# A three-stage attention and expert kernel on one core: where its made weights are split, staged and loaded

## The chip, the cores and the metric

The kernel runs on one NeuronCore of one Trainium2 chip. The metric is the time of one execution in device microseconds, as the median of several runs; a profile is one further execution taken by the hardware profiler. TensorE (PE in the profile) multiplies matrices, VectorE (DVE), ScalarE (ACT) and GpSimd (POOL) work elementwise, and SyncE (SP) issues nearly all transfers here, in program order. Each engine runs its own instructions in order and waits on semaphores for the others.

## The reference

Attention over 8 heads and 8 batches between 512 rows x and 32 state rows, both ways, gives 544 rows for each batch. They are laid side by side (4608 tokens, 512 features) and go through two expert layers, all in float32:

```python
def _moe_ref(x, w_gate, w_val, w_out):          # 512 -> 1536 -> 512
    gate = 1.0 / (1.0 + np.exp(-(x @ w_gate)))
    val = x @ w_val
    return (gate * val @ w_out)

def _moe2_ref(x, w_in, w_out):                  # 512 -> 2048 -> 512
    h = x @ w_in
    g = np.where(h >= 1, h, np.where(h <= -1, 0.0, (h + 1) ** 2 / 4))
    return (g @ w_out)
```

## The kernel before, in words

Every float32 product is three products of a high part and a remainder (hi x hi, hi x lo, lo x hi). So each operand is *split*: ScalarE writes the high part (a copy to the type of the product), VectorE subtracts it from the source and leaves the remainder in place. Several of the large products use a scheme of seven products of sums in place of eight (M1 to M7), for which sums of blocks of the weights and of the activations are made first.

The order of the work is written out by hand. The stages that the change touches, in order of time:

**The value stage, `gated(1, None, hooks)`.** Gate and value product for the second four batches, in 24 units i (L609 on TensorE). A unit uses both PSUM buffers of one of two sets, by turns; `evac1` empties unit i during unit i+1: for even i ScalarE's sigmoid (L638), for odd i VectorE's product (L640), after which POOL makes sums (L220) and `put_h` (L620, its transfer is L622) stores the pieces to `h7_dram`, some of them two units later (`late_st`). Pair products for later units (`m_pair`, L576; ScalarE L588, VectorE L594) and a preparation of raw weights (`weights.join`, L166 and L170) run in between. Into this stage `hooks` puts, by unit: `combos_wo` (L879), which loads rows of `w_out`, makes block sums and stores seven pieces to `wc_dram`; `load_wc`, `high_wc`, `low_wc` (L858 to L878), which load a piece's weights in three parts, and split them, for M1 and M5; and the first three chunks of the next stage's activations (`load_h7`, L916).

**The output product, `out7` (L948), 42 steps n.** Step n takes product j = PP[n // 3 % 7] and chunk c = n % 3. Chunk n+5 is loaded, chunk n+2 is split (L927, L220), then come the 12 matmuls. Weights of the later products are loaded and split in between (`todo`). M1, M5, M2 and M4 have weights in the tiles `wo_0` to `wo_11`, three each, in the order of `HR4`; tiles 6 and 7 also serve `evac1` as scratch, tiles 8 to 11 serve `combos_wo`.

**The state units, `gated_s(m)`, m = 0 to 11 (L1010).** The same gate and value product for the 256 state rows: 24 matmuls (L225 to L227) with weights `ws`, then sigmoid (L1019), product (L1020), split, and for odd m a difference with its split. In the loop (L1898 to L1908) each turn loads unit m+3's weights, runs `gated_s(m)`, splits the weights of unit m+1 (L1004 and L220), runs the `todo` of that turn, and from m = 3 on adds 12 matmuls of the output product for the state rows (`out1_s`, L1044). The `todo` prepares the input weights 0 to 3 of the next stage (`load_wi`, `sums_wi`, `high_wi`, `low_wi`, L1064 to L1092: two blocks of `w_in`, four sums, a split; the sums lie in one scratch tile `wst`) and loads and sums the first inputs y.

**The input product, `unit(b, m)` (L1298).** Ten blocks of four units: with weights 0 to 3, and then with 4 to 7, over the batch pairs 0, 1, 2, the state rows ("s") and pair 3. A unit is seven pieces, and after each piece `tick` runs what `plan` put there. Weights 4 to 7 are prepared as above, one after the other, in the fifth and sixth block (L2023 to L2026); y's sums and remainders for the next block are on POOL.

After it, the second output product (L1366 to L1368) takes the rest of the span.

## Time and profile before

| | us |
|---|---|
| median of 3 runs | 1450.81 (1450.1 to 1451.48) |
| the profiled execution | 1451.23 |
| its span, first to last instruction | 1449.4 |
| TensorE's matmuls busy | 1376.6 (95% of the span) |
| VectorE busy | 978.3 (67%) |
| ScalarE busy | 770.6 (53%) |
| GpSimd busy | 332.5 (23%) |

Busy times are unions of an engine's instructions; matmuls are pipelined, so a busy TensorE can still run slower than at its best. "Clock" is the TensorE clock that was granted, as a share of full speed. A row of waits gives for whom, on whom, the total, the number of times and the longest. Idle time counts only where it holds up the engine that sets the end.

### The profile page before, as it was taken

What the parts mean: (1) busy time and instruction counts of PE and PEld (TensorE: products, weight loads), DVE (VectorE), ACT (ScalarE), POOL (GpSimd) and SP (SyncE); (2) the same over time, 40 slices, a digit from 0 to 9 for tenths busy, and PEclk for the clock granted to TensorE, in tenths of its full rate; (3) what the DMA queues carried; (4) which work ended last, traced back from release to release, by engine and by line L of the source; (5) the groups of instructions that cost most, each with busy time, mean ns of one, the idle gap of its engine ahead of it and who ended that gap; (6) DMA issues with size and microseconds to landing.
All of it is one profiled execution on the core that took longest, in us unless ns stands there. A gap on an engine that the chain in (4) does not pass through costs nothing. (4 is left out here: it accounts for less than half of the span.)

```text
span 1449.4 us, 23550 instructions
## 1 busy us (share of the span) xinstructions
PE 1376.6 (95%) x8956; PEld 1168.1 (81%) x8956; DVE 978.3 (67%) x1377; ACT 770.6 (53%) x1138; POOL 332.5 (23%) x207
## 2 busy tenths in 40 slices
PE   8999999999999989996779999889999999999997
PEld 5677787787677768886668887668889999999997
DVE  6666766774476657454566666986668887877775
ACT  7655556654333445432347786768876444444432
POOL 3000000000053350000027777588741000000000
PEclk9999999999999999997889999999999999999999
DMA  7478897787499898765235555546668534433332
GB/s 254 150 257 287 289 338 239 246 283 260 166 335 341 305 310 307 239 213 169 61 109 202 200 230 197 201 161 233 236 230 319 175 123 141 138 124 117 121 127 88
DMA packets 179634, 308.80 MB, mean 213 GB/s; under 512 B 15040, under 2 KB 101824, under 8 KB 179008
## 3 DMA queue, kind: packets, MB, share of 16 engines
q1 hardware_dynamic: 178712, 306.50, 62.0%
q8 instruction: 70, 1.15, 0.3%
q10 hardware_dynamic: 808, 0.79, 0.2%
q14 instruction: 44, 0.36, 0.1%
HBM read 184.29 MB, written 122.95 MB: 212 GB/s over the span
## 5 line engine op out<-in xcount | busy, mean ns | idle before, releaser
L1298 PE MATMUL u<-yc,wt 128*128 128x512 f32 x1344 | 312.1, 393 | 20.9 <-DVE sg L1276 13.7
L1298 PEld LDWEIGHTS u<-yc,wt 128*128 128x128 f32 x1344 | 253.8, 190 | 78.4 <-DVE sg L1276 14.4
L609 PE MATMUL ps<-at_hi,M 128*128 128x512 f32 x768 | 244.6, 394 | 2.5 <-DVE M L594 2.0
L609 PEld LDWEIGHTS ps<-at_hi,M 128*128 128x128 f32 x768 | 144.9, 189 | 52.1 <-issue 18.4
L609 PE MATMUL ps<-at_lo,M 128*128 128x512 f32 x384 | 150.6, 392 | 1.8 <-DVE at_lo L405 1.8
L1368 PE MATMUL o<-wt,hc 128*128 128x256 f32 x476 | 134.8, 283 | 0.7 <-DVE hc L1415 0.7
L1366 PE MATMUL o<-w,hc 128*128 128x256 f32 x476 | 134.7, 283 | 0.0
L1367 PE MATMUL o<-w,hc 128*128 128x256 f32 x476 | 134.7, 283 | 0.0
L1367 PE MATMUL o<-wt,hc 128*128 128x256 f32 x476 | 134.7, 283 | 0.0
L1368 PE MATMUL o<-w,hc 128*128 128x256 f32 x476 | 134.7, 283 | 0.0
L1366 PE MATMUL o<-wt,hc 128*128 128x256 f32 x476 | 134.7, 283 | 0.0
L1411 ACT ACTIVATE hc<-hc 128x512 fp32r<-128x512 f32 (+1 forms) x108 | 64.9, 603 | 129.9 <-DMA hc<-hd_dram 117.3
L1220 POOL TENSOR_TENSOR yc<-yr,yc 128x1024 fp32r<-128x1024 f32 x49 | 119.6, 2475 | 24.5 <-ACT yc L1217 24.5
L594 DVE TENSOR_TENSOR M<-ps,M 128x1024 fp32r<-128x1024 f32 x48 | 56.5, 1219 | 88.1 <-ACT M L588 88.1
L1258 DVE SCALAR_TENSOR_TENSOR sg<-u,sg 128x512 f32<-128x512 f32 x96 | 66.3, 690 | 61.3 <-ACT u L1257 60.2
L1411 ACT ACTIVATE hc<-hs 128x512 fp32r<-128x512 f32 (+1 forms) x144 | 80.0, 598 | 50.5 <-DVE hs L1408 49.9
L1256 ACT ACTIVATE u<-sg,half 128x512 f32<-128x512 f32 x96 | 66.3, 691 | 70.2 <-DVE sg L1276 68.5
L220 POOL TENSOR_TENSOR sa<-sa 128x512 f32<-128x512 f32 x12 | 17.5, 1479 | 361.2 <-DVE sa L640 355.7
L220 POOL TENSOR_TENSOR w2c<-w2c 128x256 f32<-128x256 f32 (+2 forms) x40 | 43.9, 1111 | 227.6 <-ACT yc L1217 218.7
L1415 DVE TENSOR_TENSOR hc<-hs,hc 128x512 fp32r<-128x512 f32 (+1 forms) x144 | 90.3, 660 | 5.3 <-ACT hc L1411 5.2
L1368 PEld LDWEIGHTS o<-wt,hc 128*128 128x128 f32 x476 | 91.4, 192 | 0.9 <-DVE hc L1415 0.9
L1366 PEld LDWEIGHTS o<-wt,hc 128*128 128x128 f32 x476 | 91.4, 192 | 0.0
(195 smaller groups left out, 3042.9 us busy)
## 6 DMA issues: line engine op xcount, KB each, us to landing
hd_dram<-sg SPq DMA_DIRECT2D x64, 512.0 KB, 4.5
hc<-hd_dram SPq DMA_DIRECT2D x96, 256.0 KB, 4.3
hq<-h_dram SPq DMA_DIRECT2D x39, 512.0 KB, 5.3
yr<-y_dram SPq DMA_DIRECT2D x32, 512.0 KB, 6.6
wraw<-in_moe_w_out_dram SPq DMA_DIRECT2D x28, 512.0 KB, 5.2
h_dram<-sg SPq DMA_DIRECT2D x24, 512.0 KB, 4.3
oh_lo<-h_dram SPq DMA_DIRECT2D x24, 512.0 KB, 5.8
w2c_dram<-w2c SPq DMA_DIRECT2D x12, 896.0 KB, 6.0
```

The source lines that it names most:

```text
L220: eng.tensor_tensor(out=o, in0=a, in1=b, op=op)
L594: nc.vector.tensor_tensor(out=M[:, 1], in0=ps, in1=f32(M[:, 0]), op=ALU.subtract)
L609: nc.tensor.matmul(out=ps[bp][:, b2], lhsT=M[:, l, b2, c], rhs=a[:, b2], start=(hq == 0 and j == 0), stop=(hq == 1 and j == 2),)
L1220: low_on.tensor_tensor(out=t[:, 1, :n], in0=src, in1=f32(t[:, 0, :n]), op=SUB)
L1256: nc.scalar.activation(out=s, in_=c, func=AF.Relu, bias=half, scale=0.5)
L1258: return lambda: nc.vector.scalar_tensor_tensor(out=o, in0=s, scalar=1.0, in1=c, op0=ALU.min, op1=ALU.max)
L1298: nc.tensor.matmul(out=pm[j], lhsT=a, rhs=b, start=not more and k == 0 and i == 0, stop=k == 1 and i == 2, skip_group_check=more,)
L1366: nc.tensor.matmul(out=ps, lhsT=wh, rhs=vh, start=start and i == 0, stop=False)
L1367: nc.tensor.matmul(out=ps, lhsT=wh, rhs=vl, start=False, stop=False)
L1368: nc.tensor.matmul(out=ps, lhsT=wl, rhs=vh, start=False, stop=last)
L1411: nc.scalar.activation(out=get(j)[0], in_=raw(j), func=AF.Copy)
L1415: nc.vector.tensor_tensor(out=lo, in0=raw(j), in1=f32(hi), op=SUB)
```

## The change

- **State units:** unit m+2's weights are split in turn m, not unit m+1's. The scratch tile of the input weights gets a second buffer (every other unit's lies in `hsp`), the two state results share one tile `evs`.
- **Input weights 4 to 7** are loaded, summed and split earlier by `finish_wi`: two in the value stage (in the tiles `wo_8` to `wo_11`), two in the output product (in a pool `wg` of their own). Both parts are stored to `wi_dram`, and the input product loads them as they are, with one transfer of 14 KB a partition.
- **Output product:** `HR4` is M1, M5, M4, M2, so that M2 has tiles 9 to 11; its load and split come in units 20 and 23 of the value stage. Chunks 3 to 7 are loaded before the stores that the last unit of the value stage left, chunk 8 after them. The combinations move to earlier units, and only four of their seven pieces are stored; M1, M2 and M4 are read from the raw rows (`wof_dram`, one tensor now), two rows of 1 KB.
- **Layout:** `h7_dram` is piece first, so a chunk's load reads 4 KB in a row for each partition, where it read two rows of 2 KB; M2's and M3's common store becomes two rows of 2 KB.
- The state rows' input (`load_xs`) is loaded and split six steps later; the pools of the state units open at step 28, not 2.

```diff
@@ -107,8 +107,8 @@
     h_dram = tc.dram_tile([128, NM1, 4, S], F32, name="h_dram")
-    h7_dram = [tc.dram_tile([128, NQ, 7, S], F32, name=f"h7_dram_{p}") for p in range(2)]
-    wc_dram = tc.dram_tile([128, 7, NQ, 256], F32, name="wc_dram")
+    h7_dram = [tc.dram_tile([128, 7, NQ, S], F32, name=f"h7_dram_{p}") for p in range(2)]
+    wc_dram = tc.dram_tile([128, 4, NQ, 256], F32, name="wc_dram")
     xs_dram = tc.dram_tile([128, 4, NSB], F32, name="xs_dram")
@@ -119,7 +119,8 @@
     ]
-    wof_dram = {i: tc.dram_tile([128, 512], F32, name=f"wof_dram_{i}") for i in range(NM1)}
+    wof_dram = tc.dram_tile([128, NM1, 512], F32, name="wof_dram")
+    wi_dram = {m: tc.dram_tile([128, 14, 256], F32, name=f"wi_dram_{m}") for m in range(4, 8)}
     w2_dram = [tc.dram_tile([128, 512], F32, name=f"w2_dram_{i}") for i in range(NM2)]
@@ -618,7 +619,7 @@
     def put_h(p, q, j, a, n=1, due=None):
-        o = h7_dram[p][:, q, HS[j]] if n == 1 else h7_dram[p][:, q, HS[j] : HS[j] + n]
+        o = h7_dram[p][:, HS[j], q] if n == 1 else h7_dram[p][:, HS[j] : HS[j] + n, q]
         f = lambda: nc.sync.dma_start(out=o, in_=a)
@@ -628,7 +629,7 @@
             if v == 0 and mm == 0:
-                sa_t[t] = sgp.tile([128, 3, 512], F32, tag="sa", name="sa", bufs=4)
+                sa_t[t] = (sgp, sgq)[t].tile([128, 3, 512], F32, tag="sa", name="sa", bufs=2)
             elif v == 0:
@@ -730,7 +731,8 @@
         prev()
-        flush()
+        if not bg:
+            flush()
@@ -743,14 +745,14 @@
         def dst(a=None):
-            return wo_tiles(i) if a is None else wof_dram[i]
+            return wo_tiles(i) if a is None else wof_dram[:, i]
...
     def load_wo(i):
-        nc.sync.dma_start(out=f32(wo_tiles(i)[1]), in_=wof_dram[i])
+        nc.sync.dma_start(out=f32(wo_tiles(i)[1]), in_=wof_dram[:, i])
@@ -852,7 +854,9 @@
-    HR4 = (M1, M5, M2, M4)
+    HR4 = (M1, M5, M4, M2)
+    WR = {M1: (0, 0), M2: (1, 0), M4: (1, 1)}
+    WS = {M5: 0, M7: 1, M6: 2, M3: 3}
     wc_t = {}
@@ -863,9 +867,13 @@
         for p in range(3):
+            if j in WR:
+                k, v = WR[j]
+                o = wof_dram[:, 4 * p + k : 4 * p + k + 3 : 2, 256 * v : 256 * v + 256]
+            else:
+                o = wc_dram[:, WS[j], 2 * p : 2 * p + 2]
             nc.sync.dma_start(
-                out=f32(wc_t[j][1][p]),
-                in_=wc_dram[:, WI[j], 2 * p : 2 * p + 2].rearrange("p q f -> p (q f)"),
+                out=f32(wc_t[j][1][p]).rearrange("p (q f) -> p q f", q=2), in_=o
             )
@@ -883,7 +891,7 @@
             for i in range(2):
-                nc.sync.dma_start(out=box[i], in_=wof_dram[2 * q + i])
+                nc.sync.dma_start(out=box[i], in_=wof_dram[:, 2 * q + i])
@@ -894,15 +902,10 @@
         def store():
-            for t, o in zip(box, (slice(0, 4, 3), slice(1, 3), slice(4, 6))):
+            for o, a in enumerate((box[0][:, 256:], box[2][:, :256], box[2][:, 256:], box[3][:, :256])):
                 stores.append(
-                    lambda t=t, o=o: nc.sync.dma_start(
-                        out=wc_dram[:, o, q], in_=t.rearrange("p (s f) -> p s f", s=2)
-                    )
+                    lambda o=o, a=a: nc.sync.dma_start(out=wc_dram[:, o, q], in_=a)
                 )
-            stores.append(
-                lambda: nc.sync.dma_start(out=wc_dram[:, 6, q], in_=box[3][:, :256])
-            )
@@ -920,7 +923,7 @@
         h7_t[n] = t
-        nc.sync.dma_start(out=f32(t[:, 1]), in_=h7_dram[p][:, 2 * c : 2 * c + 2, HS[j]])
+        nc.sync.dma_start(out=f32(t[:, 1]), in_=h7_dram[p][:, HS[j], 2 * c : 2 * c + 2])
@@ -1047,7 +1050,7 @@
         if q == NQ - 1:
-            t = hsp.tile([128, 2, NSB], F32, tag="evs", name="evs", bufs=2)
+            t = hsp.tile([128, 2, NSB], F32, tag="evs", name="evs", bufs=1)
             if half == 0:
@@ -1061,9 +1064,63 @@
+    def finish_wi(m, tiles):
+        box = []
+
+        def r(i):
+            return box[0][1][:, 256 * i : 256 * i + 256] if len(box[0]) == 2 else pieces(i)
+
+        def parts():
+            if len(box[0]) == 2:
+                return [(box[0][0][:, :1792], box[0][1][:, :1792])]
+            n = (512, 512, 512, 256)
+            return [(box[0][p][:, :k], box[0][4 + p][:, :k]) for p, k in enumerate(n)]
+
+        def pieces(i):
+            return box[0][4 + i // 2][:, 256 * (i % 2) : 256 * (i % 2) + 256]
+
+        def load():
+            box.append(tiles())
+            for n, (i, h) in enumerate(((0, 0), (0, 1), (1, 1), (1, 0))):
+                c = slice(256 * h, 256 * h + 256)
+                nc.sync.dma_start(out=f32(r(n)), in_=wir_dram[2 * m + i][:, c])
+
+        def sums():
+            a = [f32(r(i)) for i in range(7)]
+            tt(nc.vector, a[4], a[0], a[3])
+            tt(nc.vector, a[3], a[3], a[2], ADD)
+            tt(nc.vector, a[5], a[3], a[0])
+            tt(nc.vector, a[6], a[1], a[5])
+
+        def high():
+            for hi, lo in parts():
+                nc.scalar.activation(out=hi, in_=f32(lo), func=AF.Copy)
+
+        def low():
+            for hi, lo in parts():
+                tt(nc.vector, lo, f32(lo), f32(hi))
+
+        def store():
+            o = 0
+            for p, (hi, lo) in enumerate(parts()):
+                n = hi.shape[1] // 256
+                for l, a in enumerate((hi, lo)):
+                    stores.append(
+                        lambda l=l, a=a, o=o, n=n: nc.sync.dma_start(
+                            out=wi_dram[m][:, 7 * l + o : 7 * l + o + n],
+                            in_=f32(a).rearrange("p (s f) -> p s f", s=n),
+                        )
+                    )
+                o += n
+
+        return load, sums, high, low, store
+
     def load_wi(m):
         t = w_t[m] = w_tile()
-        wst_t[m] = wst.tile([128, 4, 256], F32, tag="wst", name="wst")
+        if m >= 4:
+            nc.sync.dma_start(out=f32(t).rearrange("p l s f -> p (l s) f"), in_=wi_dram[m])
+            return
+        wst_t[m] = (hsp if m % 2 else wst).tile([128, 4, 256], F32, tag="wst", name="wst")
         nc.sync.dma_start(
@@ -1786,6 +1843,7 @@
+    sgq = pool("sgq", side="right", stack=st_a)
     mp = pool("mp1", side="right", stack=st_a)
@@ -1796,15 +1854,26 @@
-    for q in range(NQ):
+    for q, i in enumerate((0, 1, 3, 4, 6, 7)):
         load, sums, store = combos_wo(q)
-        hook(2 * q, load)
-        hook(2 * q + 2, sums)
-        hook(2 * q + 3, store)
+        hook(i, load)
+        hook(i + 2, sums)
+        hook(i + 2, store)
+
+    def wi_pieces():
+        t = [wo_tiles(8 + i) for i in range(4)]
+        return [a[0] for a in t] + [a[1] for a in t]
+
+    for m, i in ((4, 10), (5, 15)):
+        for k, f in enumerate(finish_wi(m, wi_pieces)):
+            hook(i + (0, 1, 2, 2, 3)[k], f)
+    for k, j in enumerate((M1, M5, M2)):
+        hook((13, 14, 20)[k], load_wc, j)
     for k, j in enumerate((M1, M5)):
-        hook(15 + k, load_wc, j)
         for p in range(3):
-            hook(17 + 3 * k + p, lambda j=j, p=p: (high_wc(j, p), low_wc(j, p)))
+            hook((18, 19, 20, 21, 21, 22)[3 * k + p], lambda j=j, p=p: (high_wc(j, p), low_wc(j, p)))
+    for p in range(3):
+        hook(23, lambda p=p: (high_wc(M2, p), low_wc(M2, p)))
     hook(20, load_h7, 0)
@@ -1817,18 +1886,26 @@
-    st_l, st_sb, st_w, st_e = (ExitStack() for _ in range(4))
+    st_l, st_sb, st_w, st_e, st_g = (ExitStack() for _ in range(5))
     hq = pool("hq", stack=st_l)
...
-    for k, j in enumerate(PP[2:]):
-        do(3 * k + (k == 0), load_wc, j)
+    for k, j in enumerate(PP[3:], 1):
+        do(3 * k, load_wc, j)
         for p in range(3):
...
             do(3 * k + 4, low_wc, j, p)
+
+    def wi_whole():
+        t = wgp.tile([128, 2, 1792], F32R, tag="wg", name="wg", bufs=2)
+        return [t[:, 0], t[:, 1]]
+
+    for m, n in ((6, 14), (7, 20)):
+        for k, f in enumerate(finish_wi(m, wi_whole)):
+            do(n + (0, 3, 4, 4, 5)[k], f)
@@ -1839,18 +1916,24 @@
     global_xs = []
-    do(20, load_xs)
-    do(23, lambda: nc.scalar.activation(out=global_xs[0], in_=f32(global_xs[1]), func=AF.Copy))
-    do(24, lambda: tt(nc.vector, global_xs[1], f32(global_xs[1]), f32(global_xs[0])))
+    do(26, load_xs)
+    do(28, lambda: nc.scalar.activation(out=global_xs[0], in_=f32(global_xs[1]), func=AF.Copy))
+    do(29, lambda: tt(nc.vector, global_xs[1], f32(global_xs[1]), f32(global_xs[0])))
     for m in range(3):
...
         do(36 + 2 * m, low_ws, m)
-    load_h7(3)
-    load_h7(4)
+    for n in range(3, 8):
+        load_h7(n)
+    flush()
+    load_h7(8)
     for n in range(42):
-        if n + 5 < 42:
+        if n == 28:
+            st_g.close()
+            hsp = pool("hsp", side="right", stack=st_sb)
+            wsps = [pool("wsp", side="right", stack=st_w, bufs=3)]
+        if 8 < n + 5 < 42:
             load_h7(n + 5)
@@ -1858,6 +1941,7 @@
             f()
+        flush()
         if n + 2 < 42:
@@ -1866,8 +1950,7 @@
             wcx = pool("wcx", stack=st_l)
-            hsp = pool("hsp", side="right", stack=st_sb)
-            wsps = [pool("wsp", side="right", stack=st_w, bufs=3)]
+            wgp = pool("wgp", side="right", stack=st_g)
         evac7(n)
@@ -1886,7 +1969,7 @@
-    wi = {m: wi_steps(m) for m in range(8)}
+    wi = {m: wi_steps(m) for m in range(4)}
     todo = {}
@@ -1899,9 +1982,9 @@
         gated_s(m)
-        if 0 < m and m + 1 < NM1:
-            high_ws(m + 1)
-            low_ws(m + 1)
+        if m + 2 < NM1:
+            high_ws(m + 2)
+            low_ws(m + 2)
         for f in todo.pop(m, ()):
@@ -2021,9 +2104,7 @@
     for i in range(4):
-        t = start[4] + 9 + 7 * i + 7 * (i == 3)
-        for k, n in enumerate((0, 5, 6, 7, 8)):
-            plan(t + n, wi[4 + i][k])
+        plan(start[4] + 9 + 7 * i + 7 * (i == 3), lambda i=i: load_wi(4 + i))
     for i in range(3):
...
         plan(t, lambda i=i: load_w2(i))

```

## Rows read from the trace of the kernel before

**Rows 1.** Stage windows: length, busy us by engine (xinstructions), PEclk, DMA share, GB/s

```profile
445.00:523.00 78.00, 78.00 (x461) 58.42 (x441) 51.89 (x49) 33.86 (x42) 35.46 (x25) 1.00 0.91 315
...
522.80:646.60 123.80, 117.84 (x506) 96.35 (x505) 71.93 (x68) 56.38 (x62) 8.00 (x6) 0.97 0.81 268
...
541.70:548.60 6.90, 5.74 (x13) 4.22 (x14) 5.30 (x6) 4.66 (x7) 0.00 (x0) 0.51 1.00 347
...
646.50:735.40 88.90, 64.80 (x391) 60.51 (x390) 42.02 (x66) 26.12 (x44) 0.00 (x0) 0.81 0.36 107
...
734.70:740.40 5.70, 5.70 (x50) 5.70 (x48) 3.22 (x8) 2.67 (x5) 0.00 (x0) 1.00 0.02 3
```

**Rows 2.** Waits of TensorE, whole span: us in total, times, longest

```profile
PE ps L225 <- ACT ws L1004: 13.6, 9, 2.5
...
PE u L1298 <- DVE sg L1276: 13.7, 6, 4.6
...
PE ps L948 <- ACT hq L927: 4.6, 1, 4.6
```

**Rows 3.** Waits of SyncE's queue, 500 to 552, then 646 to 741 us

```profile
SPq L866 <- DMA h_dram<-wo: 4.7, 2, 3.2
...
SPq L1070 <- DVE wt L220: 41.3, 3, 17.8
```

**Rows 4.** Timeline of the output product: start, length, engine, line, what, idle

```profile
539.38 2.01 ACT L873 ACTIVATE wo<-wo 128x512 fp32r<-128x512 f32 x3 [5.66 <-DMA wo<-wc_dram]
...
541.29 1.99 ACT L927 ACTIVATE hq<-hq 128x1024 fp32r<-128x1024 f32 x2
```

**Rows 5.** Timeline of the state units

```profile
650.01 0.42 DVE L1020 TENSOR_TENSOR sgs<-sgs,ps 128x256 f32<-128x256 f32 x1 [2.06 <-ACT sgs L1019]
...
702.49 0.42 DVE L1020 TENSOR_TENSOR sgs<-sgs,ps 128x256 f32<-128x256 f32 x1 [1.74 <-ACT sgs L1019]
...
705.58 1.23 DVE L220 TENSOR_TENSOR ws<-ws 128x1024 fp32r<-128x1024 f32 x1 [0.52 <-ACT ws L1004]
...
712.38 0.42 DVE L1020 TENSOR_TENSOR sgs<-sgs,ps 128x256 f32<-128x256 f32 x1 [4.44 <-ACT sgs L1019]
...
714.23 1.23 DVE L220 TENSOR_TENSOR ws<-ws 128x1024 fp32r<-128x1024 f32 x1 [0.52 <-ACT ws L1004]
...
735.36 0.42 DVE L1020 TENSOR_TENSOR sgs<-sgs,ps 128x256 f32<-128x256 f32 x1 [1.20 <-ACT sgs L1019]
...
742.20 3.12 SPq L1055 DMA_DIRECT2D y_dram<-evs  x2
...
745.12 2.47 PE L1298 MATMUL u<-yc,wt 128*128 128x512 f32 x5 [4.52 <-ACT yc L1217]
```

**Rows 6.** Groups of instructions in the state units: busy us, mean ns, idle

```profile
L220 DVE TENSOR_TENSOR wst<-wst,wt 128x256 f32<-128x256 f32 x8 | 3.4, 425 | 0.3
...
L220 DVE TENSOR_TENSOR wt<-wst,wt 128x1024 fp32r<-128x1024 f32 x3 | 3.7, 1218 | 0.0
...
L220 DVE TENSOR_TENSOR wt<-wt 128x768 fp32r<-128x768 f32 x3 | 2.9, 951 | 0.0
...
L220 DVE TENSOR_TENSOR yr<-yr 128x1024 f32<-128x1024 f32 x4 | 4.8, 1218 | 0.0
...
L1086 ACT ACTIVATE wt<-wst 128x1024 fp32r<-128x1024 f32 x4 | 4.2, 1058 | 8.3 <-DVE wst L220 8.3
```

**Rows 7.** Page, DMA issues: count, KB each, us to landing

```profile
hd_dram<-sg SPq DMA_DIRECT2D x64, 512.0 KB, 4.5
```

**Rows 8.** Input product's matmuls by windows: PE, PEld, PEclk, DMA share, GB/s

```profile
778.52:816.60 38.08, 38.08 (x169) 31.54 (x168) 1.00 0.56 204
...
894.78:969.82 75.04, 60.79 (x253) 47.65 (x252) 0.98 0.49 172
```

**Rows 9.** VectorE's groups, 875 to 956 us

```profile
L220 DVE TENSOR_TENSOR wst<-wt,wst 128x256 f32<-128x256 f32 x8 | 12.7, 1583 | 0.1
```

**Rows 10.** Timeline of VectorE in the value stage

```profile
454.89 1.40 DVE L220 TENSOR_TENSOR wo<-wo 128x256 f32<-128x256 f32 x1
```

## The prediction, made before the change was built

> **What bounds the kernel now.** I read the stages first, then the waits of TensorE, then, in each stage with waits, what the waited-for engine was doing. A stage is bounded by TensorE where the windows show no gap in its busy time, and by something else where they do. The value stage (second half batch, up to 522.8) has none in its last 78.00 us. The output product with chunks (522.8 to 646.6) is busy 117.84 of 123.80 us, and the state units (646.5 to 735.4) only 64.80 of 88.90, at a mean granted clock of 0.81 [rows 1]. The list of waits names the causes: weights of the state units (ACT ws 13.6 us), the chunk of the output product (ACT hq 4.6, once), and VectorE's sums in the input product (DVE sg 13.7, six times) [rows 2]. Those three are what the change goes at; the rest of the span is TensorE's own work, and is worth nothing to it.
>
> **Output product: one chain of waits goes.** The second input M2's weights share tiles 6 and 7 with scratch of the value stage. SyncE held their load until the scratch had been stored (4.7 us [rows 3]). ScalarE, in order, then split M2's weights from 539.38 and only at 541.29 the chunk that TensorE stood for [rows 4]. After that stop the clock was granted at 0.51 for 6.90 us [rows 1], the 1.2 GHz level, which costs half of it, 3.4 us. The change gives M2 the tiles 9 to 11, loads it in unit 20 of the value stage, splits it in unit 23, and issues chunks 3 to 7 before the late stores. I take the whole wait and its half clock: -(4.6 + 3.4) = **-8.0**. What is late next is chunk 8, which now waits on SyncE for M2's own last store; only the six late stores stand behind it, and step 8 comes over 20 us into the stage. VectorE gets three remainders of M2 ahead of chunk 1's; if they run slow beside POOL, up to 5 us come back, so the bounds are -9 and -3.
>
> **State units: the splits leave TensorE's loop.** Now, unit m+1's weights are split after unit m's sigmoid, product and splits, so TensorE waits for that chain and then adds its own unit. From the product's start to the end of the weights' remainder the chain takes 706.81 - 702.49 = 4.3 us in an odd unit (it has the difference too) and 715.46 - 712.38 = 3.1 in an even one [rows 5]. Splitting unit m+2 there lets TensorE run unit m+1 meanwhile. Its floor is then 12 x 24 + 8 x 12 = 384 matmuls up to the last product; 48 take 5.70 us at full clock [rows 1], so 46 us. But the in-order chain on ScalarE and VectorE remains, and I find it longer than that. Between the first product and the last one (units 0 to 10) it needs: five odd units 5 x 4.3 = 21.6; five even ones 5 x 3.1 = 15.4; unit 10, with no weights left to split, about 1.3 (a product, a split and its remainder of 0.4 each); three sets of input-weight sums, 3 x 4 x 0.42 = 5.1, and ScalarE's split of them, 3 x 1.06 = 3.2, which stands before the next sigmoid; three sets of remainders, 3 x (1.22 + 0.95) = 6.5; four sums of y, 4 x 1.22 = 4.9 [rows 6]. That is 58.0 against 735.36 - 650.01 = 85.4 measured [rows 5], -27.4. Loads of units 3 to 5 still queue behind wide y loads at the start, so I take **-26**. The bounds: VectorE's own busy time in the stage is 42.02 us [rows 1], which with no wait at all inside the chain would give -43; and no gain, below. The second change here is small in code and needed: SyncE stood 41.3 us for the one scratch tile of the input weights [rows 3], with state weights queued behind it; a second tile removes that, and without it the loads would come too late for a split two ahead.
>
> The clock speaks against this sum. The stage's mean is 0.81 [rows 1], between the levels of 1.2 and 2.4 GHz, so it spent some 40% at the lower one; my chain leaves TensorE waiting some 1 to 2 us in most units. The Trainium skill (TensorE: Matmul & The Clock Gate, HAM oscillation) says that a loop whose waits return in every tile can start every tile at the half clock. By that rule the stage would be bounded by TensorE and hardly change, a rival below. I stay with the chain, because a TensorE at half clock lets the chain catch up, the next wait goes, and the clock returns.
>
> The tail from the last product to the first input product (735.36 to 745.12) is a chain of its own that the change leaves, but for one thing: the two state outputs now share one tile, so the second copy out of PSUM waits until the first one's store has landed. It is issued at 742.20 [rows 5]. A 512 KB store lands in 4.5 us [rows 7], this one is half that size. Bounds 0 (landed in time) and +2.5; I take **+0.7**, since most of a short landing has passed when the copy comes up.
>
> **Input product: four weights' preparation goes.** Undisturbed, four units take 38.08 us, so six take 57.12; the six from 894.78 took 75.04 [rows 8], 17.9 too long, half clock included. In that stretch VectorE makes the weights of units 4 to 7, with 8 of the sums alone taking 12.7 us at 1583 ns each, beside POOL [rows 9]. Afterwards one load brings them ready made. It is 1.84 MB instead of 0.52, four times, 5.3 MB more over 75 us, on DMA engines that are 0.49 busy there [rows 8]; each is issued 12 to 19 pieces ahead of its unit (a unit has seven). I take **-17**, bounds -18 and -12 (if a late load or slow y sums keep a third).
>
> **Value stage: the work moved in.** Two of the four sets are made here, at units 10 to 14 and 15 to 19; M2's split is added in unit 23, and the combinations of the output weights move forward. A set costs VectorE four sums and four remainders, 1.7 + 2.2 us by the free durations [rows 6], but a 256-wide sum beside POOL takes 1.40 [rows 10]. From 445 to 523 VectorE is 51.89 of 78.00 us busy [rows 1], so the time is there. The order is the problem: VectorE comes to the sums one unit after SyncE was to load their inputs, and SyncE takes those loads behind the stores of that unit. If VectorE stands there for a landing, the remainders of the pair products behind it hold PSUM that TensorE needs for its next unit. Bounds 0 (loads land in time) and +10 (two landings of 4.5, exposed, and a little more); I take **+4**, half of a landing for each set. DMA there is 0.91 busy at 315 GB/s [rows 1], so full load is about 346. The window gets some 4 MB more on 24.6 (two loads of 0.52, two stores of 1.84, M2's 0.79, less 1.5 of combinations): 28.6 MB, or 83 us of DMA in 78. That lateness of 5 us lands on the first chunks, whose loads the change puts ahead of the stores, and five steps of lead take it.
>
> The other two sets are made in the output product, where VectorE is busy 71.93 of 123.80 us [rows 1] and two chunks ahead: nothing. The 4 KB rows, the combined tensors and the later pools: nothing, none stands in a chain above; 1 KB rows of three raw weight loads likewise.
>
> **Sum.** The profiled execution took 1451.23 us, 0.4 above the median of the runs. -8.0 - 26 + 0.7 - 17 + 4 = -46.3: 1404.9, or **1404.5** against the median.
>
> **Rivals.**
> 1. *The half clock keeps the state units* (chance 0.08). 384 matmuls at twice 0.119 are 91 us: no gain there, rather +3. For it: 0.81 now. Against: above. Time 1404.5 + 29 = 1434.
> 2. *VectorE stalls the value stage* (0.12). Two exposed landings, each followed by a spell of half clock, +18 instead of +4: 1418.
> 3. *The input product's waits stay* (0.07): it wouldn't do what it says if POOL's y sums, not the weights, are what VectorE is slow beside. The gain there falls to 6: 1415. Against: other units with the same POOL work run at 38.08 per four [rows 8].
> 4. *VectorE and ScalarE overlap better* than my chain in the state units (0.06): -38 there, 1392.
> 5. *Slower* (0.03): SyncE is in order, and in the value stage each of eight load groups (six combinations, two sets) may stand behind the landing of a store issued just before it, with job and pair weights queued behind. To eat 46 us each must cost TensorE 5.8, more than a landing of 4.5 [rows 7]; it decides from there: some 1455.
>
> **Numbers.** Forecast 0.64. The range 1394 to 1426 takes in the forecast with its bounds, and rivals 2 and 3; left out are rival 1, 4 and 5, 0.17. About 0.2% is what a measurement of this kernel tells from no change. Faster 0.96, same 0.01, slower 0.03.
>
> **What would show it.** Right: in the state units the waits for ws are gone or under half, VectorE's last product comes near 709, and SyncE no longer waits for wt; no wait of TensorE for hq near step 5; six units of 57 to 58 us at what is now 895; a few short waits around units 13 and 18 of the value stage. Wrong: a clock near 0.6 throughout the state units; waits for M or ps of several us in the value stage; a wait on the copy before the first input product of over 2 us more.

## The result, and the profile after

The changed kernel takes 1413.59 us (median of 4 executions, 1407.81 to 1414.27) beside 1451.14 for the kernel before on the same chip: a ratio of 0.9729, 95% interval 0.9699 to 0.9759. That is 37.6 us less. The forecast was 1404.5, range 1394 to 1426. The profiled execution took 1414.27, its span is 1412.5.

I cut both spans at the same places: last matmul of the first batches' output product (its end, 364.4 before, 364.5 after), first matmul of `out7`, its last one, first and last of the input product. The last columns split the output product: TensorE starts a matmul every 0.227 us there (the median), so 504 need 114.4 us, and what each group of steps takes beyond that pace is listed, in us. All kernels of this study stand here, so that each can be read by stage; "time" is the median, and a profile is one execution of it.

| kernel | time | value | output | state + tail | input | steps 0-3 | 4-6 | 7-13 | 21-29 |
|---|---|---|---|---|---|---|---|---|---|
| before | 1451.1 | 158.4 | 123.9 | 98.4 | 351.2 | 1.2 | 8.3 | 0.0 | 0.0 |
| changed | 1413.6 | 165.5 | 124.0 | 71.0 | 334.8 | 0.7 | 0.0 | 5.0 | 3.7 |
| one | 1440.1 | 165.3 | 124.8 | 97.6 | 332.9 | 1.3 | 0.0 | 6.4 | 2.6 |
| wst1 | 1412.5 | 165.6 | 124.7 | 71.7 | 332.4 | 0.5 | 0.0 | 7.2 | 2.6 |
| nowi | 1419.8 | 154.8 | 121.5 | 72.1 | 353.3 | 1.8 | 0.0 | 5.3 | 0.0 |
| w67 | 1412.8 | 154.8 | 124.1 | 70.7 | 342.0 | 2.2 | 0.0 | 5.0 | 2.4 |
| rows2 | 1414.0 | 166.1 | 123.5 | 70.9 | 335.2 | 0.0 | 0.0 | 5.9 | 2.6 |
| set2 | 1409.5 | 157.7 | 128.7 | 71.5 | 332.5 | 5.1 | 0.0 | 6.7 | 2.4 |
| wi7 | 1412.8 | 163.9 | 122.9 | 71.4 | 332.5 | 0.1 | 0.0 | 7.0 | 1.3 |
| m6 | 1410.3 | 164.6 | 121.6 | 72.4 | 334.7 | 0.7 | 0.0 | 4.4 | 2.0 |
| ahead | 1412.0 | 165.1 | 122.3 | 70.7 | 332.3 | 4.6 | 0.0 | 0.0 | 3.2 |
| mix | 1408.6 | 165.5 | 120.0 | 70.7 | 333.3 | 0.8 | 2.8 | 0.0 | 1.9 |
| best | 1404.9 | 157.3 | 125.3 | 70.9 | 332.6 | 9.4 | 0.0 | 0.0 | 1.5 |
| best2 | 1404.4 | 158.4 | 123.0 | 71.4 | 333.4 | 7.6 | 0.2 | 0.0 | 0.7 |

Before to after: value stage +7.1, output product +0.1, state units and tail -27.5, input product -16.5. The windows of the changed kernel, as in [rows 1] and [rows 8] (length, busy us by engine, clock, DMA share, GB/s), first the last 78 us of the value stage, then the output product, the state units and six units of the input product:

```profile
452.00:530.00 78.00, 71.30 (x393) 52.82 (x394) 54.02 (x56) 34.50 (x46) 34.67 (x24) 0.96 0.86 303
530.00:654.00 124.00, 118.67 (x507) 96.61 (x506) 80.89 (x77) 57.22 (x61) 10.41 (x6) 0.97 0.85 301
653.80:709.90 56.10, 46.79 (x364) 44.13 (x362) 36.45 (x60) 24.54 (x42) 0.00 (x0) 0.99 0.55 169
...
869.00:926.10 57.10, 57.10 (x253) 47.30 (x252) 36.36 (x55) 44.37 (x66) 47.79 (x24) 1.00 0.94 331
```

The value stage, which had no gap in its last 78 us before, now has 6.7 us of them. The state units run at a clock of 0.99 in this window; a spell of 3.4 us at the lower level (709.3 to 712.7) falls behind its end, and up to the last product (715.2) the mean is 0.97. The six units have no gap left, where [rows 8] had 14 us of them (the window shown begins 30 matmuls early; counted by matmuls the same six run from 876.02 to 933.14, 57.1 us as well), and VectorE is busy 36.36 of 57.10 us without the weights. The list of TensorE's waits (total, times, longest) names what is new:

```profile
PE ps L610 <- DVE M L595: 5.7, 1, 5.7
PE ps L228 <- DVE ws L221: 5.4, 8, 0.8
PE u L1355 <- ACT yc L1274: 5.2, 1, 5.2
PE ps L226 <- ACT ws L1007: 3.8, 4, 1.6
PE ps L951 <- DVE hq L221: 2.6, 2, 1.8
PE ps L951 <- ACT hq L930: 2.3, 1, 2.3
PE u L1355 <- DVE sg L1333: 2.3, 2, 2.0
...
PE ps L610 <- DVE oh_lo L641: 1.7, 1, 1.7
```

Against [rows 2], ScalarE's `ws` fell from 13.6 us to 3.8 and VectorE's `sg` from 13.7 to 2.3. One wait for `hq` of 4.6, with two short ones for VectorE beside it (1.4 in all), has become three of 2.3, 1.8 and 0.8, and two waits in the value stage, of 5.7 and 1.7, are new. With three of them (the 5.7 from 487.13 on, the 2.3 from 552.63 and the 1.8 from 604.23) the clock went to its lower level, 1.2 GHz; these are the windows of those stretches:

```profile
490.80:497.70 6.90, 4.90 (x12) 3.84 (x13) 6.83 (x11) 3.06 (x6) 0.00 (x0) 0.51 0.47 176
555.70:559.10 3.40, 2.89 (x7) 2.31 (x8) 3.40 (x6) 1.20 (x2) 0.00 (x0) 0.50 1.04 396
606.90:610.30 3.40, 3.40 (x10) 2.62 (x9) 3.40 (x3) 3.40 (x4) 0.00 (x0) 0.50 1.05 431
```

The timeline of the changed kernel (start, length, engine, line, what, idle before it) gives two of the causes. VectorE stood 12.29 us for the loads of weight 5 in the value stage, with the small part of M behind them in its queue, and 5.95 us for those of weight 7 in the output product, with a chunk's low part behind:

```profile
483.43 2.08 SPq L1086 DMA_DIRECT2D wo<-wir_dram  x4
...
489.80 0.42 DVE L221 TENSOR_TENSOR wo<-wo,wo 128x256 f32<-128x256 f32 x1 [12.29 <-DMA wo<-wir_dram]
...
491.53 2.35 DVE L595 TENSOR_TENSOR M<-ps,M 128x1024 fp32r<-128x1024 f32 x2
...
603.03 1.81 DVE L221 TENSOR_TENSOR wg<-wg 128x256 f32<-128x256 f32 x4 [5.95 <-DMA wg<-wir_dram]
604.76 1.22 DVE L221 TENSOR_TENSOR hq<-hq 128x1024 fp32r<-128x1024 f32 x1
```

The third is SyncE's. Its list of waits from 526 to 560 us starts with the load of a chunk that waits for a store:

```profile
SPq L926 <- DMA h_dram<-oh_lo: 8.9, 1, 8.9
```

and its timeline shows what that holds up: M2's last two stores go out from 531.86 and chunk 8, which reads the first of them back, at 542.07. In the 8.9 us before that SyncE issues nothing; the six late stores and M6's three weight loads (546.75) come behind.

```profile
530.50 1.31 SPq L926 DMA_DIRECT2D hq<-h_dram  x2
531.86 1.30 SPq L623 DMA_DIRECT2D h_dram<-oh_lo  x2
542.07 0.33 SPq L926 DMA_DIRECT2D hq<-h_dram  x1
542.50 0.38 SPq L623 DMA_DIRECT2D h_dram<-sa  x1
542.98 0.91 SPq L623 DMA_DIRECT2D h_dram<-wo  x2
543.98 0.89 SPq L623 DMA_DIRECT2D h_dram<-sa  x1
544.97 1.51 SPq L623 DMA_DIRECT2D h_dram<-wo  x2
546.75 1.65 SPq L875 DMA_DIRECT2D wc<-wc_dram  x3
```

ScalarE, in order, then takes M6's weights as they land and chunk 8, which had landed at 545.95, after them (553.86); TensorE has stood for it since 552.63:

```profile
550.72 0.63 ACT L881 ACTIVATE wc<-wc 128x512 fp32r<-128x512 f32 x1 [7.79 <-DMA wc<-wc_dram]
...
553.32 0.63 ACT L881 ACTIVATE wc<-wc 128x512 fp32r<-128x512 f32 x1 [0.35 <-DMA wc<-wc_dram]
553.86 1.99 ACT L930 ACTIVATE hq<-hq 128x1024 fp32r<-128x1024 f32 x2
```

### The profile page after: what moved, and what is told of

It is laid out like the page before. It is cut to its first block, busy times and chain, and to the rows that moved or that the text cites. A ratio compares the mean times of both kernels' runs of the same rounds, so it can differ in the third digit from the quotient of the medians.

```text
span 1412.5 us, 23632 instructions
## 1 busy us (share of the span) xinstructions
PE 1363.3 (97%) x8956; PEld 1157.8 (82%) x8956; DVE 958.9 (68%) x1379; ACT 770.2 (55%) x1140; POOL 330.2 (23%) x207
## 5 line engine op out<-in xcount | busy, mean ns | idle before, releaser
L1277 POOL TENSOR_TENSOR yc<-yr,yc 128x1024 fp32r<-128x1024 f32 x49 | 116.5, 2410 | 12.8 <-ACT yc L1274 12.7
L1425 PEld LDWEIGHTS o<-wt,hc 128*128 128x128 f32 x476 | 91.4, 192 | 0.8 <-DVE hc L1472 0.8
L1423 PEld LDWEIGHTS o<-wt,hc 128*128 128x128 f32 x476 | 91.4, 192 | 0.0
L1424 PEld LDWEIGHTS o<-wt,hc 128*128 128x128 f32 x476 | 91.4, 192 | 0.0
```

The lines of the kernel that those rows point to most:

```text
L1277: low_on.tensor_tensor(out=t[:, 1, :n], in0=src, in1=f32(t[:, 0, :n]), op=SUB)
L1423: nc.tensor.matmul(out=ps, lhsT=wh, rhs=vh, start=start and i == 0, stop=False)
L1424: nc.tensor.matmul(out=ps, lhsT=wh, rhs=vl, start=False, stop=False)
L1425: nc.tensor.matmul(out=ps, lhsT=wl, rhs=vh, start=False, stop=last)
```

## The experiments

Every edit is against the changed kernel. The ratios are to the kernel before, run beside each. By the totals alone only one, nowi and best2 can be told from the changed kernel (0.9699 to 0.9759); elsewhere the stages have to show it, each from one profile, and where nothing was changed steps 7 to 13 scatter from 5.0 to 7.2 us and steps 21 to 29 from 1.9 to 3.7.

**one**: the split one unit ahead again.

```diff
-        if m + 2 < NM1:
-            high_ws(m + 2)
-            low_ws(m + 2)
+        if 0 < m and m + 1 < NM1:
+            high_ws(m + 1)
+            low_ws(m + 1)
```

> The changed kernel, with only the split of the state units' weights put back to one unit ahead (their loads still run three units ahead, into the two buffers). Theory of the prediction: the split's distance carries nearly all of the gain of the state units; their stretch from first to last product, 57.9 us in the changed kernel and 85.4 before, goes back to 76 to 85 us, and the whole to 1432 to 1441 us. Rival: the second buffer, by which the loads come earlier, carries the gain; then the stretch is 58 to 66 us and the whole at most 1422.

1440.09 us (ratio 0.9925, 0.9907 to 0.9944), as the theory has it: first to last product 84.1 us, state units and tail 97.6 instead of 71.0. The split's distance is worth 26.6 of the 27.5 us. In the waits of this kernel ScalarE's and the landings' `ws` are back, and the stage's window shows the clock of before:

```profile
PE ps L226 <- ACT ws L1007: 11.8, 8, 2.2
PE ps L228 <- DVE ws L221: 7.0, 10, 0.8
PE ps L226 <- DMA ws<-wf_dram: 5.9, 2, 3.6
```

```profile
654.90:747.70 92.80, 68.09 (x433) 63.58 (x431) 45.19 (x73) 28.68 (x48) 0.00 (x0) 0.83 0.34 103
```

**wst1**: one scratch tile for the input weights.

```diff
-        wst_t[m] = (hsp if m % 2 else wst).tile(
+        wst_t[m] = wst.tile(
```

> The changed kernel, with one buffer instead of two for the state units' weights as they come in (and for the input product's first sets, which use the same two). Theory: with the split two ahead and loads three ahead, one buffer lets a load be issued only when the split before it is done, so the landing of about 4.5 us stands in every unit; the stretch from first to last product of the state units is 62 to 72 us instead of 57.9, and SyncE's wait for those buffers, 2.1 us in the changed kernel, is over 15 us; the whole takes 1418 to 1427. Rival: the split's distance carries all; then the stretch stays within 1.5 us of 57.9 and the whole within 3 us of 1413.6.

1412.49 us (0.9737, 0.9721 to 0.9754). My theory fell and the rival held: 58.6 us from first to last product, 0.7 more. SyncE's wait did come back (23.5 us in place of 2.1), and it cost next to nothing: with the split two ahead and the loads three ahead, state weights behind that wait still land in time. The expectation calls this tile a buffer of the state units' weights; it holds input weights and their sums, and the state weights' loads only stand behind its own on SyncE.

```profile
SPq L1127 <- DVE wt L221: 23.5, 3, 11.1
```

**nowi**: all four weights made in the input product again.

```diff
...
-    for m, i in ((4, 10), (5, 15)):
-        for k, f in enumerate(finish_wi(m, wi_pieces)):
-            hook(i + (0, 1, 2, 2, 3)[k], f)
...
-    for m, n in ((6, 14), (7, 20)):
-        for k, f in enumerate(finish_wi(m, wi_whole)):
-            do(n + (0, 3, 4, 4, 5)[k], f)
...
-        plan(start[4] + 9 + 7 * i + 7 * (i == 3), lambda i=i: load_wi(4 + i))
+        t = start[4] + 9 + 7 * i + 7 * (i == 3)
+        for k, n in enumerate((0, 5, 6, 7, 8)):
+            plan(t + n, wi[4 + i][k])
```

> The changed kernel, with weights 4 to 7 of the input product made and split in the input product again (none of it in the value stage or the output product). Theory: the input product takes 16.5 us more (about 351), the value stage 7 us less (about 73 as in the kernel before), the output product some 3 us less, since weights 6 and 7 no longer stand in VectorE's queue there; the whole takes 5 to 8 us more, about 1420. Rival: the value stage's 7 us come from the loads of chunks and of output weights and not from the sets; then the value stage stays at 80 us, and the whole takes 1427 to 1431.

1419.8 us (0.9784, 0.9769 to 0.9799), 6.2 over the changed kernel, within the theory. By stage: input product +18.5 (TensorE's waits for `sg` at 13.6 us, as before), value stage -10.7, output product -2.5. So the early making, as it stands here, earns 18.5 us and pays 13 of them back. The value stage without the sets is 3.6 us shorter than before: the rest of the change gains there, and why stays open.

**w67**: only weights 4 and 5 made in the input product again, 6 and 7 early. The edit is the first and, for two of four units, the last hunk of the one above.

> The changed kernel, with weights 4 and 5 of the input product made and split in the input product again and only 6 and 7 ahead, in the output product. With all four put back the value stage was 10.9 us shorter, the output product 2.5 us shorter and the input product 18.5 us longer. Theory: what the value stage lost comes from the two sets made in it, so all 10.9 us come back here, and the input product pays only for these two, about half, 8 to 10 us; the output product keeps weight 7's wait and loses 0 to 1 us. The whole takes 1410 to 1413 us, so the two early sets are worth nothing or less. Rival: the transfers of these sets only shift the stretch in which the DMA engines are full, and the output product takes on what the value stage gives back; then the whole takes 1418 us or more.

1412.83 us (0.9738, 0.9716 to 0.9759): no difference from the changed kernel that these runs can tell. The value stage gives back all of the 10.7 us, the input product takes 7.3, a little less than expected. The two sets made in the value stage are worth nothing where they stand; the gain in the input product that is kept comes from weights 6 and 7.

**rows2**: the 2 KB rows of `h7_dram`.

```diff
-    h7_dram = [tc.dram_tile([128, 7, NQ, S], F32, name=f"h7_dram_{p}") for p in range(2)]
+    h7_dram = [tc.dram_tile([128, NQ, 7, S], F32, name=f"h7_dram_{p}") for p in range(2)]
...
-        nc.sync.dma_start(out=f32(t[:, 1]), in_=h7_dram[p][:, HS[j], 2 * c : 2 * c + 2])
+        nc.sync.dma_start(out=f32(t[:, 1]), in_=h7_dram[p][:, 2 * c : 2 * c + 2, HS[j]])
```

> The changed kernel, with only the layout of the h7 buffer in DRAM put back, so that a chunk is loaded in rows of 2 KB instead of 4 KB. Theory: the transfers' rows are beside other work, and TensorE's waits in the output product come from the order of issues and not from what the transfers carry; the output product stays within 1.5 us of 123.85 and the whole within 3 us of 1413.6. Rival: the stage is bound by its transfers (the DMA engines are busy .85 of it), and rows of half the size lengthen it by 5 us or more.

1413.97 us (0.9746, 0.9732 to 0.9761), the output product 123.5: the length of the rows costs nothing here, as the prediction had it.

**set2**: weight 5's work one unit later, M2's weights loaded after chunk 1.

```diff
-            hook(i + (0, 1, 2, 2, 3)[k], f)
-    for k, j in enumerate((M1, M5, M2)):
+            hook(i + (0, 1, 2, 2, 3)[k] + (m == 5 and k > 0), f)
+    for k, j in enumerate((M1, M5)):
...
     hook(21, load_h7, 1)
+    hook(21, load_wc, M2)
```

> The changed kernel, with only the sums, splits and store of the second set of input weights (weight 5) one unit later in the value stage, and M2's output weights, which take the set's buffers, loaded after chunk 1 of the output product instead of before it. Theory: the second set's sums stand on VectorE until its loads land, this holds back the small split of M, and TensorE's single longest wait in the value stage (5.67 us before the split of M) and the half clock after it come from that. Then that wait is under 1 us, the stage ends 6 to 9 us earlier after its start than in the changed kernel, and the whole takes about 1405 us (ratio to the kernel before .968). Rival: VectorE is full there in any order, and the wait turns up elsewhere in the stage; then the stage keeps its length and the time stays within 2 us of 1413.6.

1409.54 us (0.9716, 0.9702 to 0.9731). The cause is settled: the wait for M is gone and the value stage 7.8 us shorter, with both sets still made in it. But the 1405 us that were expected weren't reached: the output product is 4.7 us longer, 4.4 of them at steps 0 to 3, because ScalarE now takes M2's weights, which land (523.38) after chunk 1 (522.31), ahead of it (TensorE waits from 525.02):

```profile
523.46 2.08 ACT L881 ACTIVATE wo<-wo 128x512 fp32r<-128x512 f32 x3 [5.02 <-DMA wo<-wof_dram]
525.44 1.04 ACT L930 ACTIVATE M<-M 128x1024 fp32r<-128x1024 f32 x1
```

**wi7**: weight 7's work one step later.

```diff
-            do(n + (0, 3, 4, 4, 5)[k], f)
+            do(n + (0, 3, 4, 4, 5)[k] + (m == 7 and k > 0), f)
```

> The changed kernel, with only the sums, splits and store of weight 7 one step later in the output product. Theory: VectorE stands 5.95 us for weight 7's loads (10 us from issue to landing) with chunk 24's low part queued behind it, and this is TensorE's 1.80 us wait there and the half clock after it; then both are gone and the output product is about 3.5 us shorter, the whole about 1410. Rival: the transfers of this stretch are late whatever VectorE does, and TensorE then waits for another chunk by as much; the time stays within 1.5 us of 1413.6.

1412.84 us (0.9734, 0.9716 to 0.9752). At its place it does what the theory says: steps 21 to 29 lose 1.3 us in place of 3.7, and the chunk's low part stands before the sums (601.77, then 602.91). But 3.7 was the high end: in eight other runs without this edit, with weight 7 made here, these steps lost 1.9 to 3.2, and in the three with it (here, best, best2) 0.7 to 1.5. So the edit is worth 1 to 2 us, not the 3.5 expected, and the total stays where the rival had it, though no other chunk waits by as much. In this execution steps 7 to 13 lost 7.0 us besides.

**m6**: M6's weights split one step later, behind chunk 8.

```diff
-            do(3 * k + 3, high_wc, j, p)
-            do(3 * k + 4, low_wc, j, p)
+            do(3 * k + 3 + (k == 1), high_wc, j, p)
+            do(3 * k + 4 + (k == 1), low_wc, j, p)
```

> The changed kernel, with only the high and low parts of M6's output weights one step later in the output product (at steps 7 and 8; the product that uses them is step 9). Theory: at step 8 TensorE waits 2.32 us for ScalarE's high part of chunk 8, because ScalarE, in order, first stands for M6's late weights; with those behind the chunk that wait is gone or under .5 us, .77 us of a wait for VectorE with it and some 1.5 us of half clock, so the output product takes about 119.5 us instead of 123.85, and the whole 4 us less, about 1409.5. Rival: chunk 8 is itself late, being loaded behind M2's last store; then the wait stays at 1.5 us or more, and the time within 1.5 us of 1413.6. Second rival: M6's own weights are now what the next step waits for; then a wait of about 2 us stands at step 9.

1410.32 us (0.9719, 0.9703 to 0.9736). The second rival in place and size: chunk 8 is in time now (split at 545.53), and TensorE stands one step on, at step 9, which uses M6's weights (`wc`). It stands 1.21 us for ScalarE's part of chunk 9, whose load went out behind the same stop, at 547.89, and 0.77 for M6's weights:

```profile
555.69 0.49 PE L951 MATMUL ps<-hq,wc 128*128 128x512 f32 x1 [1.21 <-ACT hq L930]
556.95 1.40 PE L951 MATMUL ps<-hq,wc 128*128 128x512 f32 x2 [0.77 <-DMA wc<-wc_dram]
```

Steps 7 to 13 lose 4.4 us, little less than 5.0. The total is near the theory's 1409.5, but not by its mechanism. Turning the two round on ScalarE doesn't mend it: SyncE's stop makes both late.

**ahead**: the stores first, then chunks 3 and 4, then one chunk a step, as before.

```diff
-    for n in range(3, 8):
-        load_h7(n)
     flush()
-    load_h7(8)
+    load_h7(3)
+    load_h7(4)
...
-        if 8 < n + 5 < 42:
+        if n + 5 < 42:
```

> The changed kernel, with the chunk loads of the output product behind the late stores again, in the order of the kernel before (the stores first, then chunks 3 and 4, and one chunk a step). Theory: this part of the change moved a wait and removed none: the waits of 2.32 and .77 us at chunk 8 go, a wait of about 4.6 us before step 5 comes back, and the output product stays within 2 us of 123.85, the whole within 3 us of 1413.6. Rival: loading the chunks ahead is worth the 8 us that the prediction gave it, and something else took them back; then the whole takes 1419 us or more.

1412.01 us (0.973, 0.9716 to 0.9745). Right in the total and in that the loss at steps 7 to 13 goes (5.0 to 0.0); wrong in that the wait of 4.6 us would come back. Steps 4 to 6 lose nothing; 4.6 us are lost at steps 0 to 3, with a wait of 1.46 for chunk 3 and half clock after it. So the old wait went with M2's weights, which have other tiles and an earlier load, and the five chunks ahead weren't needed for it: they spare 3.9 us at steps 0 to 3 and cost 5.0 at steps 7 to 13.

**mix**: chunks 3 and 4, then the stores, then one chunk a step.

```diff
-    for n in range(3, 8):
-        load_h7(n)
+    load_h7(3)
+    load_h7(4)
     flush()
-    load_h7(8)
...
-        if 8 < n + 5 < 42:
+        if n + 5 < 42:
```

> The changed kernel, with the order of issues at the start of the output product between the two tried: chunks 3 and 4, then M2's last stores, then one chunk a step from chunk 5 on, ahead of the late stores only for chunk 5. Theory: five chunks ahead hold M2's last stores back, on which chunk 8 waits, and none ahead leaves chunk 3 behind stores that wait for VectorE (1.46 us in the run with the stores first); with two ahead both waits are under 1 us, the output product takes 119 to 121.5 us instead of 123.85, and the whole 1409 to 1411. Rival: the transfers are so dense here that one of the chunks is late in any order; then the stage takes 122 us or more and the whole 1412 to 1415.

1408.63 us (0.972, 0.9693 to 0.9747), the output product 120.0. Waits of 1.02 and 0.76 remain at step 6, and steps 7 to 13 lose nothing. SyncE's longest stop in this stretch is now 3.4 us, in place of 8.9:

```profile
SPq L926 <- PE ps L951: 3.6, 2, 2.3
SPq L969 <- ACT ev L986: 3.4, 1, 3.4
```

**best**: set2, mix and wi7 together, and M2's weights split in steps 2 and 3.

```diff
-    for p in range(3):
-        hook(23, lambda p=p: (high_wc(M2, p), low_wc(M2, p)))
+    for p in range(3):
+        do(2, high_wc, M2, p)
+        do(3, low_wc, M2, p)
```

> Three edits together: weight 5's work one unit later, M2's weights loaded after chunk 1 and split at steps 2 and 3 of the output product (behind chunk 1's split, where in the run with weight 5 later they stood in front of it); two chunks ahead of M2's last stores instead of five; weight 7's work one step later. Theory: the value stage keeps the 7.8 us that the first edit gave, the output product no longer gives 4.7 of them back and loses another 2 to 4 of its waits; the whole takes 1400 to 1404 us (ratio to the kernel before .965 to .968), better than every kernel so far. Rival: the DMA engines are full from 520 to 560 us and set the pace; then the output product's first steps wait as long as the value stage ends earlier, and the whole takes 1408 to 1411.

1404.93 us (0.9685, 0.9667 to 0.9703), 0.9 over the theory's bound and well under the rival's. The value stage keeps its gain (157.3), and steps 4 to 20 lose nothing. Steps 0 to 3 lose 9.4: TensorE waits 3.92 and 1.41 us for chunk 2 and has the lower clock from 530.4 to 540.7. Chunk 2 reads what M1's last sums have just stored, and an output product that starts 8 us earlier comes to it too soon.

**best2**: the same, with M2's weights loaded behind chunk 2, split in steps 4 and 5.

```diff
-    hook(21, load_wc, M2)
     hook(23, load_h7, 2)
+    hook(23, load_wc, M2)
```

> The run of three edits, with M2's output weights loaded behind chunk 2 instead of behind chunk 1, and split at steps 4 and 5 of the output product. In the run of three edits the remaining wait is at step 2: 3.92 us for ScalarE's high part of chunk 2 and 1.41 for its low part. Chunk 2's load (issued 526.13) had waited 2.5 us on SyncE for the last stores of M1, and these were issued right behind the three loads of M2's weights (517.55 to 518.89, landed 523.99). Theory: the weights' transfers ahead of those stores make them late; behind chunk 2 they cost nothing, the two waits shrink to 1 to 3 us in all, and the whole takes 1401 to 1403.5 us. Rival: the chain from M1's last sums over the store to the load sets chunk 2 whatever goes before; then the wait stays over 4 us and the time within 1 us of 1404.9. Second rival: M2's weights are now late for step 6, and a wait of 2 us or more stands there.

1404.37 us (0.9679, 0.9666 to 0.9692): the first rival in the main. Chunk 2's load goes out 2.2 us earlier (523.98, was 526.13), but the waits at step 2 are still 2.67 and 1.60 us. That fits a chain from M1's last sums over a store and a load, but no run tests it by itself: the load took 5.9 us to land (529.90), so dense transfers may have their part. The interval lies wholly below the changed kernel's 0.9699, so this version beats both kernels, by some 7 us (from the ratios) and 47 us.

## Why the prediction was right, and where it was wrong

**State units: right, by the reason given.** The chain of ScalarE and VectorE was added up to 58.0 us from the first product to the last; measured:

```profile
657.28 0.42 DVE L1023 TENSOR_TENSOR sgs<-sgs,ps 128x256 f32<-128x256 f32 x1 [2.06 <-ACT sgs L1022]
...
715.20 0.41 DVE L1023 TENSOR_TENSOR sgs<-sgs,ps 128x256 f32<-128x256 f32 x1
...
724.12 0.68 DVE L1057 COPY evs<-ps 128x512 f32<-128x512 f32 x1
```

57.9 us. The terms agree too, not only their sum. From one product to the next VectorE's timeline gives 21.2 us for the five odd units and 15.4 for the five even ones (21.6 and 15.4 forecast), 9.6 for the input weights' sums with ScalarE's split (8.3), 6.0 for their remainders (6.5), 4.5 for y's sums (4.9) and 1.2 for unit 10 (1.3). So the bound was the chain, and of the two values in the text (-27.4 from the chain, -26 taken) the chain's own was the better. One supporting claim was false: that without the second scratch tile the loads would come too late (wst1: 0.7 us).

The half-clock rival fell. The stage ran at 0.97 up to the last product, with one spell at the lower level, although TensorE waited twelve times in it, up to 1.65 us each. In the run with the split one ahead, with waits of about 2.2 us in every second unit and up to 3.6, the clock was 0.83. The Trainium skill (TensorE: Matmul & The Clock Gate, HAM oscillation) describes a loop in which each tile's work is shorter than the wait for the next. Here a unit's work, 24 to 36 matmuls or an estimated 2.9 to 4.3 us at full clock (48 take 5.70 [rows 1]), is longer than its waits, so the prediction stretched the page, and these runs don't speak against it.

**Tail: +0.7 forecast, nothing found.** From the last product to the first input product it is 9.74 us in place of 9.76. The second copy (from 724.12, above) ends 0.14 us before that product, as it ended 0.15 before it in the kernel before (744.97 and 745.12), and VectorE didn't stand for it. In two other runs (set2, one) it stood 0.25 us ahead of the copy, the profile names the copy as what the product waited for, and the tail took 10.1 us. So the shared tile costs 0 to 0.3 us; the landing was put too long, with 1.98 us measured where the trace has it (w67).

**Input product: right.** -16.5 measured, -17 forecast, and putting the work back costs 18.5.

**Value stage: the mechanism right, the size too small.** +4 stood for half a landing at each set. Weight 4's cost a wait of 1.74 us, weight 5's 5.67 and 6.9 us at the lower clock, 2.0 of them inside the wait; the stage is 7.1 us longer, inside the bounds, and the two sets cost 10.7 against the kernel without them. With weight 5's work one unit later (set2, which also moves M2's load) they cost 2.9, so most of that is one place in VectorE's order. The term left out that VectorE's stand is counted from when it arrives, not from when the load goes out: it came at 477.5 to loads that SyncE issued from 483.43 on, and could start only at 489.80. The text's own sign of being wrong, a wait for M of several us, stood here.

**Output product: the step that failed.** "I take the whole wait and its half clock: -8.0." The whole wait went: steps 4 to 6 lost 8.3 us before and nothing after. But the stage is as long as it was, for two reasons that the text had costed at nothing. It said of chunk 8 that "only the six late stores stand behind it" and that step 8 comes over 20 us into the stage. The 10 us that M2's store took to land, with five chunk loads ahead of it, stopped SyncE's issues for 8.9 us, and M6's weights were behind. That cost 5.0 us at steps 7 to 13, and nothing is lost there with fewer chunks ahead (ahead, mix). And of the two sets made in the output product it said: "nothing". Weight 7's loads took 10 to 11 us to land, VectorE stood for them, and that cost 3.7 at steps 21 to 29 (1.9 to 3.2 in other runs, nothing without the sets). 5.0 + 3.7 is what was to be gained. The bounds of -9 and -3 missed it because both ended at M2; the row that spoke against it, the DMA share of 0.81 to 1.00 [rows 1], was read for the value stage only.

Terms against measurements: -8.0 / 0.1, -26 and +0.7 / -27.5, -17 / -16.5, +4 / +7.1. The miss of 9 us is the first and the last, less some 2 us more than forecast from the second.

Of the rivals, the second (VectorE stalls in the value stage) came half true: one of its two exposed landings was followed by a spell of the lower clock. The slower one's mechanism, SyncE in order behind a store's landing, is real, but it struck once, at chunk 8.

## What to carry to other kernels

When a wait is taken off the critical path, price the next one on every in-order queue that the edit passes, above all a load that reads back a store just issued: it stops every later issue for that store's whole landing under load, not for the landing in a quiet stretch. Work moved into another stage costs what it makes *that* stage's queues stand for, so move the load earlier than the work by the landing measured there. A split moved one unit further ahead can be worth more than all else, and is priced by adding up the other engines' chain.

## What the runs showed of the hardware

- A 512 KB transfer landed in 4.5 us as a median [rows 7]; at a DMA share of 1.00 and then 0.94 (530 to 536, 536 to 542) the chunk issued at 531.25 landed at 540.76, and the store issued behind it at 531.86 at 542.02. The load that reads that store back was issued 0.05 us after its landing. The Trainium skill (DMA: Bandwidth & Descriptors, "Two DMAs through the same engine are not ordered") says that the issuing engine has to wait for the first transfer's completion before it issues the dependent one; the trace agrees, and shows the price: 8.9 us without an issue.
- The input product of kernels with the same code in it took 332.3 to 333.4 us in eight profiles and 334.7 to 335.2 in three. The difference is in the main one spell of 3.4 us at the lower clock, right after the first wait for VectorE: in the changed kernel the clock was 0.61 in the 4 us after the wait of 2.00 us, in the run "best" 1.00 after one of 2.04. So it isn't the length of that wait alone, and I know no more of it; it is some 2 us of scatter in the totals above.

```profile
736.90:740.90 4.00, 4.00 (x12) 3.11 (x12) 2.57 (x5) 2.77 (x5) 3.21 (x4) 0.61 0.43 174
```

```profile
729.10:733.10 4.00, 3.90 (x16) 2.95 (x17) 2.57 (x4) 2.27 (x4) 3.84 (x5) 1.00 0.52 214
```
